# Attention row maxima: of three products a key tile, one made of 256 keys in each row half

## Chip, core and metric

The kernel runs on one core of a Trainium2 chip. The metric is the device time of one execution in microseconds; the time shown is the median of three runs. The core has five engines that run side by side and wait for each other by semaphores: TensorE (PE, its weight loads PEld), VectorE (DVE), ScalarE (ACT), GpSimd (POOL) and SyncE (SP, which issues DMAs). TensorE writes into PSUM, eight banks of 128 rows by 512 f32 columns.

## The reference

A pre-norm transformer block on 2048 tokens of width 640, all in f32: 32 heads of width 20, then a gated feed-forward layer of width 1728.

```
h   = x + attention(layernorm(x))
out = h + ffn(layernorm(h))

scores = einsum("bhqd,bhkd->bhqk", q, k) * (Dh ** -0.5)
p = softmax(scores, axis=-1)
o = einsum("bhqk,bhkd->bhqd", p, v)
ffn(x) = (silu(x @ w_gate) * (x @ w_up)) @ w_down
```

The softmax is the exact one: the row maximum over all 2048 keys is taken off before the exponential. The maxima are computed from q and k by products of their own, ahead of the scores that they serve.

## The kernel before

The program has three stages: layer norm and projections, attention, then output projection and feed-forward. The order of the work is written out by hand; every engine runs its instructions in the order in which the program issues them.

Attention is cut into 32 units `u`: eight groups of four heads, times four chunks of 512 queries. A unit runs over 16 key tiles `kt` of 128 keys, so there are 512 tiles. The keys and queries of four heads lie in two row halves (`b`, partitions 0 to 63 and 64 to 127) of two pairs each; a head uses 60 rows, and two more rows carry the negated row maximum in two parts. A product that has 60 or 62 rows uses one half of TensorE's rows.

In a key tile (`ORDER`, a string of letters) stand:

- `s` and `S`: a score product (line 1300, `scores`), 62 rows by 128 keys against 512 queries into one bank of `ps_one`, in row half 0 and 1; two of each. ScalarE takes the exponential of each bank into `probs` (line 1306).
- `m` and `M`: a maximum product (line 274, `max_one`), 60 rows by 128 queries against 512 keys into one bank of `ps_max`, in row half 0 and 1; three in all, `m` twice in even tiles and `M` twice in odd ones. VectorE reduces each bank to one column of `mx` (line 280). They serve a later unit: the list `rest` holds 736 entries (unit, key chunk, query tile, pair), each with both halves.
- `W`: the weighing of the tile two back (line 1310, `weigh`): four heads side by side in four column strips, into the bank `acc`. After the sixteenth tile of a unit ScalarE copies `acc` to `o` (line 1320).

`ps_one` has four banks in turn, so each score of a tile waits for the exponential of the score at the same place in the tile before. `ps_max` has three; the one whose reduction came first is given out first. A bank is given out when the product that fills it is issued, and that product carries the wait. When a unit has all its maxima, `max_all` reduces the columns of `mx` to one value per row (line 287), GpSimd splits it in two parts, VectorE turns it and DMAs bring it into the queries' spare rows. `W` also carries other work by the piece, among it the preparation of feed-forward weights on GpSimd, and in the last two units products of the output projection, which take `ps_max` banks.

```
def next_max(b):
    if singles[b]:
        a = singles[b].pop(0)
        max_one(*a)
```

After some 491 tiles the maxima are used up and a tile is `sSsSW`.

Of the kernel before, what the change touches and what calls it, by code (L numbers as in the profile page):

```python
# [9 lines left out]
F32 = mybir.dt.float32  # L10
# [4 lines left out]
ALU = mybir.AluOpType  # L15
AX = mybir.AxisListType

P = 128
S = 2048
D = 640  # L20
H = 32
# [4 lines left out]
CH = 512  # L26
NC = S // CH
TPC = CH // P
# [9 lines left out]
LOWEST = -3.4028234e38  # L38
GD = G * DH

ORDER = ("WsSmmSsM", "WSsMMsSm")


@with_exitstack
def tile_block(ctx: ExitStack, tc: tile.TileContext, x, wqkv, wo, wg, wu, wd, out):
    nc = tc.nc
# [100 lines left out]
    NU = NG * NC  # L147
# [4 lines left out]
    stk = att_ctx.enter_context(tc.tile_pool(name="stk", bufs=1, side="right"))  # L152
    k_stk = [stay.tile([P, 2, S], F32R, name="k_stk0", tag="first")]
    v_stk = [stay.tile([P, NT, VG], F32, name="v_stk0", tag="second")]
    keys, queries, values = {}, {}, {}
# [24 lines left out]
    def load_keys(g, cs):  # L180

        k = keys[g] = k_stk[g % 2]
        stack(k[:, :, cs], 1, g, cs.start // CH)
# [11 lines left out]
        )  # L195

    def mx_tile(u, **tag):
        return stk.tile([P, 2, 2, TPC, NC], F32, name=f"mx{u}", **tag)

    mxs = {u: mx_tile(u) for u in range(NU) if u % NC < 2 or u == 2}  # L200

# [63 lines left out]

        return differences, maxima

    def max_one(u, kc, t, pair, b):

        ps = ps_max()  # L270
        if u not in mxs:
            mxs[u] = mx_tile(u, tag="mx_late", bufs=3)
        rows = slice(b * ROW, b * ROW + NPART)
        nc.tensor.matmul(  # L274
            ps,
            queries[u][rows, pair, t * P : (t + 1) * P],
            keys[u // NC][rows, pair, kc * CH : (kc + 1) * CH],
            start=True, stop=True,
        )
        nc.vector.tensor_reduce(  # L280
            mxs[u][:, b, pair, t, kc : kc + 1], ps, axis=AX.X, op=ALU.max
        )

    def max_all(u):

        ends[u] = stk.tile([P, G * TPC], F32, name="neg", tag="neg", bufs=2)
        nc.vector.tensor_reduce(
            ends[u], mxs[u].rearrange("p b h t k -> p (b h t) k"), axis=AX.X, op=ALU.max, negate=True
        )

    def max_parts(u):

        neg = ends[u]
        both = ends[u] = stk.tile([P, 2, G * TPC], F32R, name="neg2", bufs=2)
        nc.gpsimd.tensor_copy(both[:, 0], neg)
        nc.gpsimd.tensor_tensor(
            out=both[:, 1], in0=neg, in1=both[:, 0].bitcast(F32), op=ALU.subtract
        )
# [66 lines left out]
    with tc.tile_pool(name="pa", bufs=2) as pa:  # L365
# [21 lines left out]
        slot = [0]  # L387
# [468 lines left out]
        for c in range(NC):  # L856
# [7 lines left out]
            for j, (kind, *which) in enumerate(work):  # L864
# [31 lines left out]
                else:  # L896
# [10 lines left out]
                    def ps_max():  # L907
                        n = turn[0] % 5
                        turn[0] += 1
                        if n > 2:  # L910
                            return psum_two.tile([P, CH], F32, name="ps_max", tag="ps_two")
                        return psum.tile([P, CH], F32, name="ps_max", tag="ps_max", bufs=3)
# [4 lines left out]
                if (c, j) in ((1, 14), (1, 16), (2, 4), (3, 4)):  # L917
                    n = c if c > 1 else (j - 14) // 2
# [376 lines left out]
    def scores(u, kt, j, probs):  # L1295

        p, b = divmod(j, 2)
        rows = slice(b * ROW, b * ROW + NPART + 2)
        ps = ps_one()
        nc.tensor.matmul(  # L1300
            ps,
            keys[u // NC][rows, p, kt * P : (kt + 1) * P],
            queries[u][rows, p, :],
            start=True, stop=True,
        )
        nc.scalar.activation(probs[p][:, b, :], ps, AF.Exp, scale=scale)  # L1306
# [43 lines left out]
            )  # L1350

    todo, tail, accs, later, full, now = [], [], {}, {}, [], [0]
    singles = [[(*a, b) for a in rest] for b in range(2)]
    left = {u: sum(2 for a in rest if a[0] == u) for u in range(1, NU)}

    def next_max(b):
        if singles[b]:
            a = singles[b].pop(0)
            max_one(*a)
            left[a[0]] -= 1  # L1360
            if left[a[0]] == 0:
                full.append(a[0])

    def weigh_next():
        u, kt, probs = todo.pop(0)
        if kt == 0:
            accs[u] = psum.tile([P, CH], F32, name="acc", tag=f"ps_{last % 3}")
        weigh(u, kt, probs, accs[u])
        if kt == NT - 1:
            queues = [nc.sync] if u + 1 < NU else [nc.scalar, nc.sync]  # L1370
            tail.append((u, *row_sums(accs.pop(u), *queues)))

    extra = []
    preparing = prepare_weights()
    for u in range(NU):
        g, c = divmod(u, NC)
        if g == NG - 1 and c >= 2:
            _, first, ln, flips, _ = ahead
            extra = [*first, *ln, lambda: None, *flips]
        for kt in range(NT):  # L1380
            now[0] = u * NT + kt
            probs = [pp.tile([P, 2, CH], F32, name="probs") for _ in range(2)]
            heads = [[0, 2], [1, 3]]
            order = ORDER[now[0] % 2] if singles[0] or singles[1] else "sSsSW"
            for op in order:
                if op in "mM":
                    next_max(int(op == "M"))
                elif op in "sS":
                    scores(u, kt, heads[op == "S"].pop(0), probs)
                else:  # L1390
                    if len(todo) == 2:
                        weigh_next()
                    for f in later.pop(now[0], ()):
                        f()
                    if extra:
                        extra.pop(0)()
                    if preparing and u and kt not in (3, 4):
                        preparing.pop(0)()
                    if now[0] == (NU - NC) * NT + 8:
                        unit_ring, last_ring = weight_rings()  # L1400
# [52 lines left out]
    u, o, r = tail.pop()  # L1453
# [561 lines left out]
```

## Time and profile before

| | us |
|---|---|
| median of three runs | 2027.66 (2025.42 to 2028.07) |
| the profiled execution | 2025.84 |
| its span, first to last instruction | 2024.0 |
| TensorE busy | 2003.7 |
| VectorE busy | 1602.4 |
| ScalarE busy | 1439.9 |
| GpSimd busy | 788.5 |

The mean granted clock of TensorE is 0.999. Rows of groups give line, engine, operation, what is written from what, shape and count, then busy us, mean ns of one, and the idle time before them with what ended it. Rows of windows give the stretch, then the busy time of PE, PEld, DVE, ACT and POOL with counts, the clock, the DMA share and GB/s. Rows of the timeline give start, length, engine and line; "x4" merges neighbours, and the end of a matmul is modelled, so starts are what to read on PE. Rows of one source line give the duration in ns as least, median and most. An instruction's weights are loaded by a row of PEld, which carries its waits.

### The profile page before, as it was taken

What the parts mean: (1) busy time and instruction counts of PE and PEld (TensorE: products, weight loads), DVE (VectorE), ACT (ScalarE), POOL (GpSimd) and SP (SyncE); (2) the same over time, 40 slices, a digit from 0 to 9 for tenths busy, and PEclk for the clock granted to TensorE, in tenths of its full rate; (3) what the DMA queues carried; (4) which work ended last, traced back from release to release, by engine and by line L of the source; (5) the groups of instructions that cost most, each with busy time, mean ns of one, the idle gap of its engine ahead of it and who ended that gap; (6) DMA issues with size and microseconds to landing.
All of it is one profiled execution on the core that took longest, in us unless ns stands there. A gap on an engine that the chain in (4) does not pass through costs nothing. (4 is left out here: it accounts for less than half of the span.)

```text
span 2024.0 us, 39916 instructions
## 1 busy us (share of the span) xinstructions
PE 2003.7 (99%) x14302; PEld 1242.0 (61%) x14302; DVE 1602.4 (79%) x2816; ACT 1439.9 (71%) x2827; POOL 788.5 (39%) x1166
## 2 busy tenths in 40 slices
PE   8999999999999999999999999999999999999999
PEld 6999995333334333333333333345588888888888
DVE  5687778888888898988988988875387666676677
ACT  4678878999999999999999999987633222212221
POOL 7464423334443453443400011011155444744555
PEclk9999999999999999999999999999999999999999
DMA  7877563443634544435412132221258654974642
GB/s 245 255 254 261 180 207 83 117 146 95 189 104 139 153 143 128 155 128 173 148 58 68 36 85 58 80 63 56 59 182 296 218 189 154 353 268 159 204 150 95
DMA packets 199340, 310.35 MB, mean 153 GB/s; under 512 B 53744, under 2 KB 87856, under 8 KB 198120
## 3 DMA queue, kind: packets, MB, share of 16 engines
q1 hardware_dynamic: 192552, 284.21, 43.7%
q0 software_dynamic: 6496, 23.60, 3.9%
q8 instruction: 114, 1.87, 0.4%
q14 instruction: 82, 0.67, 0.1%
q10 hardware_dynamic: 96, 0.00, 0.0%
HBM read 208.11 MB, written 99.19 MB: 152 GB/s over the span
## 5 line engine op out<-in xcount | busy, mean ns | idle before, releaser
L1306 ACT ACTIVATE probs<-ps_one 128x512 f32<-128x512 f32 x2048 | 1056.6, 615 | 61.2 <-PE ps_one L1300 35.3
L280 DVE TENSOR_REDUCE mx<-ps_max 128x1 f32<-128x512 f32 x1472 | 924.9, 684 | 106.3 <-PE ps_one L1300 77.6
L1300 PE MATMUL ps_one<-q_stk,k_stk 62*128 62x512 f32 x2048 | 583.3, 450 | 0.7 <-DMA q_stk<-m_d 0.6
L1310 PE MATMUL acc<-probs,v_stk 128*32 128x512 f32 x4096 | 546.2, 606 | 0.0
L1300 PEld LDWEIGHTS ps_one<-q_stk,k_stk 62*128 62x128 f32 x2048 | 248.7, 184 | 441.2 <-ACT probs L1306 416.7
L274 PE MATMUL ps_max<-k_stk,q_stk 60*128 60x512 f32 x1472 | 374.9, 426 | 1.0 <-DVE mx L261 0.9
L274 PEld LDWEIGHTS ps_max<-k_stk,q_stk 60*128 60x128 f32 x1472 | 272.8, 186 | 26.9 <-DVE mx L280 2.1
L1693 DVE TENSOR_TENSOR tmp<-ps_a,tmp 128x512 f32<-128x512 f32 x208 | 141.2, 689 | 122.4 <-PE ps_a L1478 96.7
L261 DVE TENSOR_REDUCE mx<-ps_max 128x2 f32<-128x512 f32 x288 | 180.7, 685 | 63.9 <-PE ps_max L239 58.7
L1310 PEld LDWEIGHTS acc<-probs,v_stk 128*32 128x32 f32 x4096 | 80.6, 108 | 179.0 <-issue 168.0
L251 ACT ACTIVATE ps_max<-ps_max 128x512 f32<-128x512 f32 x288 | 151.6, 584 | 42.9 <-PE ps_max L239 40.3
L1572 PE MATMUL ps_b<-halves,yp 128*128 128x320 f32 x1032 | 179.0, 308 | 1.5 <-DMA halves<-j_d 1.2
L1572 PEld LDWEIGHTS ps_b<-halves,yp 128*128 128x128 f32 x1032 | 165.2, 188 | 17.5 <-POOL yp L90 1.5
L1478 PE MATMUL ps_a<-t,units 128*128 128x512 f32 x624 | 162.5, 396 | 0.0
L90 POOL TENSOR_TENSOR yp<-y,yp 128x256 fp32r<-128x256 f32 x96 | 60.2, 627 | 189.8 <-ACT yp L89 189.8
L1478 PE MATMUL ps_a<-z,units 128*128 128x512 f32 x516 | 133.9, 394 | 0.0
L1478 PEld LDWEIGHTS ps_a<-t,units 128*128 128x128 f32 x624 | 112.6, 188 | 18.5
L1345 POOL TENSOR_TENSOR o<-o,rb 128x512 f32<-128x512 f32 x31 | 39.9, 1286 | 199.1 <-DMA q_stk<-q_d 74.1
L1577 DVE TENSOR_TENSOR h<-ps_b,h 128x320 f32<-128x320 f32 x248 | 109.9, 480 | 6.9 <-PE ps_b L1572 5.4
L643 PE MATMUL ps_one<-z_hi,w_lo 64*128 64x512 f32 x380 | 113.5, 392 | 0.0
L643 PE MATMUL ps_one<-z_lo,w_hi 64*128 64x512 f32 x380 | 112.3, 392 | 0.0
L643 PE MATMUL ps_one<-z_hi,w_hi 64*128 64x512 f32 x380 | 111.7, 393 | 0.0
(225 smaller groups left out, 2637.4 us busy)
## 6 DMA issues: line engine op xcount, KB each, us to landing
units<-w_d SPq DMA_DIRECT2D x186, 256.0 KB
w_d<-stage SPq DMA_DIRECT2D x106, 256.0 KB
halves<-j_d SPq DMA_DIRECT2D x70, 320.0 KB
j_d<-stage SPq DMA_DIRECT2D x42, 320.0 KB
k_stk<-k_d SPq DMA_DIRECT2D x64, 160.0 KB
q_stk<-q_d SPq DMA_DIRECT2D x64, 160.0 KB
raw<-k_d SPq DMA_DIRECT2D x62, 160.0 KB
raw<-q_d SPq DMA_DIRECT2D x54, 160.0 KB
```

Source lines behind the costliest of these rows:

```text
L251: nc.scalar.activation(ps, ps, AF.Relu)
L261: nc.vector.tensor_reduce(mx[:, b, :, t, kc], ps.rearrange("p (j n) -> p j n", j=2), axis=AX.X, op=ALU.max,)
L274: nc.tensor.matmul(ps, queries[u][rows, pair, t * P : (t + 1) * P], keys[u // NC][rows, pair, kc * CH : (kc + 1) * CH], start=True, stop=True,
L280: nc.vector.tensor_reduce(mxs[u][:, b, pair, t, kc : kc + 1], ps, axis=AX.X, op=ALU.max)
L643: nc.tensor.matmul(ps, a[rows], b[rows], start=(i == n == 0), stop=(i == 1 and n == last), skip_group_check=True,)
L1300: nc.tensor.matmul(ps, keys[u // NC][rows, p, kt * P : (kt + 1) * P], queries[u][rows, p, :], start=True, stop=True,)
L1306: nc.scalar.activation(probs[p][:, b, :], ps, AF.Exp, scale=scale)
L1310: nc.tensor.matmul(acc[32 * j : 32 * j + 32, :], values[u // NC][:, kt, j * VW : j * VW + 32], probs[j // 2][:, j % 2, :], start=(kt == 0) ...
L1478: nc.tensor.matmul(ps.rearrange("p (t n) -> p t n", t=TPC), w[k][:, i], z[k][:, :, j], start=(first and m == 0), stop=(last and m == len(n ...
L1572: nc.tensor.matmul(ps, a, b, start=(n == 0), stop=(n == len(pairs) - 1))
L1577: nc.vector.tensor_tensor(out=h, in0=ps, in1=h, op=ALU.add)
L1693: add = lambda out, ps, x: nc.vector.tensor_tensor(out=out, in0=ps, in1=x, op=ALU.add)
```

## The change

One of the three maximum products of a tile is split in two. `h` and `H` issue a product of 256 keys each, `h` in row half 0, `H` in row half 1, into the two halves of one bank of `ps_max`; the bank is taken at `h`, and after `H` one reduction over two groups of 256 columns writes the maxima of both halves. An entry of the list needs two such banks, one for the first 256 keys and one for the other 256. The two remaining products are one whole entry, first half 1, then half 0. Since two row halves write the same bank, `H` is made to wait until `h` has ended: a no-op on TensorE that waits for TensorE's own semaphore, and then the product.

The first 256 keys of an entry use the slot of its key chunk in `mx`; the maxima of the other 256 go to one of two extra slots per row, so `mx` grows from 4 to 6 slots for all units but the first. The extra slots are filled with the lowest f32: 16 tiles by GpSimd ahead of attention, the other 15 by VectorE when they are first used.

```diff
-ORDER = ("WsSmmSsM", "WSsMMsSm")
+ORDER, LAST_ORDER = "WhSsMsSHm", "sSsSW"
...
     def mx_tile(u, **tag):
-        return stk.tile([P, 2, 2, TPC, NC], F32, name=f"mx{u}", **tag)
+        n = NC + (2 if tag else u > 0)
+        return stk.tile([P, 2, 2, TPC, n], F32, name=f"mx{u}", **tag)
...
+    def max_product(ps, u, t, pair, b, k0, k1):
         rows = slice(b * ROW, b * ROW + NPART)
         nc.tensor.matmul(
             ps,
             queries[u][rows, pair, t * P : (t + 1) * P],
-            keys[u // NC][rows, pair, kc * CH : (kc + 1) * CH],
-            start=True, stop=True,
+            keys[u // NC][rows, pair, k0:k1],
+            start=True, stop=True, skip_group_check=True,
         )
...
+    def max_slots(u):
+        if u not in mxs:
+            mxs[u] = mx_tile(u, tag="mx_late", bufs=3)
+            nc.vector.memset(mxs[u][:, :, :, :, NC:], LOWEST)
+        return mxs[u]
...
+    def max_half(ps, i, u, kc, t, pair, b):
+        k0 = kc * CH + i * (CH // 2)
+        cols = slice(b * CH // 2, (b + 1) * CH // 2)
+        max_product(ps[:, cols], u, t, pair, b, k0, k0 + CH // 2)
+
+    def max_halves(ps, i, u, kc, t, pair):
+        slot = kc
+        if i:
+            n = halved[u, t, pair] = halved.get((u, t, pair), 0) + 1
+            slot = NC - 1 + n
         nc.vector.tensor_reduce(
-            mxs[u][:, b, pair, t, kc : kc + 1], ps, axis=AX.X, op=ALU.max
+            max_slots(u)[:, :, pair, t, slot], ps.rearrange("p (j n) -> p j n", j=2),
+            axis=AX.X, op=ALU.max,
         )
...
     def next_max(b):
-        if singles[b]:
-            a = singles[b].pop(0)
+        if not whole and rest:
+            a = rest.pop(0)
+            whole.extend((*a, i) for i in (b, 1 - b))
+        if whole:
+            a = whole.pop(0)
             max_one(*a)
...
+    def next_half(b):
+        if not halves_of and rest:
+            a = rest.pop(0)
+            halves_of.extend((i, a, []) for i in range(2))
+        if not halves_of:
+            return
+        i, a, banks = halves_of[0]
+        if not banks:
+            banks.append(ps_max())
+            max_half(banks[0], i, *a, b)
+        else:
+            nc.tensor.keepalive_nop([nc.tensor.lower_ap(banks[0])])
+            max_half(banks[0], i, *a, b)
+            max_halves(banks[0], i, *a)
+            counted(a[0], 2 * i)
+            halves_of.pop(0)
...
+    for u in range(1, NU):
+        if u in mxs:
+            nc.gpsimd.memset(mxs[u][:, :, :, :, NC:], LOWEST)
```

TensorE's order in one tile of the middle of attention, with the number behind a name telling one bank from another and the engine whose semaphore is waited for in brackets: before, the weighing, then two scores, two maximum products, two scores, a maximum product.

```order
L1310 MATMUL acc_15791<-probs_15752,v_stk1_5606 32x512 x2
L1310 MATMUL acc_15791<-probs_15753,v_stk1_5606 32x512 x2
L1300 MATMUL ps_one_15827<-q_stk_14413,k_stk1_5605 128x512 [waits Activation_49]
L1300 MATMUL ps_one_15830<-q_stk_14413,k_stk1_5605 128x512 [waits Activation_49]
L274 MATMUL ps_max_15833<-k_stk1_5605,q_stk_15434 128x512 [waits DVE_49]
L274 MATMUL ps_max_15836<-k_stk1_5605,q_stk_15434 128x512 [waits DVE_49]
L1300 MATMUL ps_one_15839<-q_stk_14413,k_stk1_5605 128x512 [waits Activation_49]
L1300 MATMUL ps_one_15842<-q_stk_14413,k_stk1_5605 128x512 [waits Activation_49]
L274 MATMUL ps_max_15845<-k_stk1_5605,q_stk_15434 128x512 [waits DVE_49]
```

The same place of the changed kernel (its lines 1338, 1328 and 272 are the weighing, the scores and the maximum products):

```order
L1338 MATMUL acc_20514<-probs_20745,v_stk1_5606 32x512 x2
L1338 MATMUL acc_20514<-probs_20746,v_stk1_5606 32x512 x2
L272 MATMUL ps_max_20810<-k_stk1_5605,q_stk_20162 128x256 [waits DVE_49]
L1328 MATMUL ps_one_20812<-q_stk_19135,k_stk1_5605 128x512 [waits Activation_49]
L1328 MATMUL ps_one_20815<-q_stk_19135,k_stk1_5605 128x512 [waits Activation_49]
L272 MATMUL ps_max_20818<-k_stk1_5605,q_stk_20162 128x512 [waits DVE_49]
L1328 MATMUL ps_one_20821<-q_stk_19135,k_stk1_5605 128x512 [waits Activation_49]
L1328 MATMUL ps_one_20824<-q_stk_19135,k_stk1_5605 128x512 [waits Activation_49]
L272 MATMUL ps_max_20810<-k_stk1_5605,q_stk_20162 128x256 [waits PE_49,PE_sequencer_49]
L272 MATMUL ps_max_20830<-k_stk1_5605,q_stk_20162 128x512 [waits DVE_49]
```

The first half product now opens the tile's products, the second stands next to last, behind the fourth score and behind the no-op, and the last whole product follows it. The whole products and the scores alternate between the halves.

VectorE's order of reductions in the changed kernel, with the two-column one (line 307) between the whole ones (line 292); before, all rows were alike:

```order
L292 TENSOR_REDUCE mx21_139<-ps_max_16066 128x1 [waits PE_49]
L307 TENSOR_REDUCE mx21_139<-ps_max_16058 128x2 [waits PE_sequencer_49,PE_49]
L292 TENSOR_REDUCE mx21_139<-ps_max_16078 128x1 [waits PE_49]
L292 TENSOR_REDUCE mx21_139<-ps_max_16102 128x1 [waits PE_49]
L307 TENSOR_REDUCE mx21_139<-ps_max_16094 128x2 [waits PE_sequencer_49,PE_49]
L292 TENSOR_REDUCE mx21_139<-ps_max_16114 128x1 [waits PE_49]
```

The bank of the two half products (16058) is taken before that of the first whole one (16066) but reduced after it. The number of reductions per tile is the same as before.

More of the change, by code (lines that the diff above doesn't have):

```diff
@@ L266, in max_four @@
         return differences, maxima
[L268 to L272, printed above, removed]
+    def max_product(ps, u, t, pair, b, k0, k1):
         rows = slice(b * ROW, b * ROW + NPART)
@@ L276, in max_one @@
             queries[u][rows, pair, t * P : (t + 1) * P],
-            keys[u // NC][rows, pair, kc * CH : (kc + 1) * CH],
-            start=True, stop=True,
-        )
+            keys[u // NC][rows, pair, k0:k1],
+            start=True, stop=True, skip_group_check=True,
+        )
+    halved = {}
+    def max_slots(u):
[3 more added lines that the diff above has]
+        return mxs[u]
+    def max_one(u, kc, t, pair, b):
+        ps, mx = ps_max(), max_slots(u)
+        max_product(ps, u, t, pair, b, kc * CH, (kc + 1) * CH)
+        nc.vector.tensor_reduce(mx[:, b, pair, t, kc : kc + 1], ps, axis=AX.X, op=ALU.max)
+    def max_half(ps, i, u, kc, t, pair, b):
[7 more added lines that the diff above has]
+            slot = NC - 1 + n
+            assert slot < max_slots(u).shape[-1]
         nc.vector.tensor_reduce(
-            mxs[u][:, b, pair, t, kc : kc + 1], ps, axis=AX.X, op=ALU.max
+            max_slots(u)[:, :, pair, t, slot], ps.rearrange("p (j n) -> p j n", j=2),
+            axis=AX.X, op=ALU.max,
         )
@@ L1352, in tile_block, with counted @@
     todo, tail, accs, later, full, now = [], [], {}, {}, [], [0]
-    singles = [[(*a, b) for a in rest] for b in range(2)]
     left = {u: sum(2 for a in rest if a[0] == u) for u in range(1, NU)}
-    def next_max(b):
-        if singles[b]:
-            a = singles[b].pop(0)
-            max_one(*a)
-            left[a[0]] -= 1
-            if left[a[0]] == 0:
-                full.append(a[0])
+    whole, halves_of = [], []
+    def counted(u, n):
+        left[u] -= n
+        if n and left[u] == 0:
+            full.append(u)
+    def next_max(b):
+        if not whole and rest:
[3 more added lines that the diff above has]
+            a = whole.pop(0)
+            max_one(*a)
+            counted(a[0], 1)
+    def next_half(b):
[14 more added lines that the diff above has]
+            halves_of.pop(0)
     def weigh_next():
@@ L1383, in tile_block @@
             heads = [[0, 2], [1, 3]]
-            order = ORDER[now[0] % 2] if singles[0] or singles[1] else "sSsSW"
-            for op in order:
+            for op in ORDER if rest or whole or halves_of else LAST_ORDER:
                 if op in "mM":
                     next_max(int(op == "M"))
+                elif op in "hH":
+                    next_half(int(op == "H"))
                 elif op in "sS":
```

## Prediction

> **What bounds the kernel now.** I read the table of windows first, because the page's shares average over stages with different limits, and the change touches one stage alone: attention with row maxima.
>
> ```profile
> 300.00:1347.00 1047.00, 1045.34 (x7386) 420.92 (x7386) 933.39 (x1552) 1015.34 (x1985) 321.95 (x526) 1.00 0.38 113
> 1347.00:1392.00 45.00, 44.94 (x288) 28.08 (x282) 31.01 (x68) 27.01 (x53) 7.42 (x5) 1.00 0.25 81
> L1306 ACT ACTIVATE probs<-ps_one 128x512 f32<-128x512 f32 x2048 | 1056.6, 615 | 61.2 <-PE ps_one L1300 35.3
> L280 DVE TENSOR_REDUCE mx<-ps_max 128x1 f32<-128x512 f32 x1472 | 924.9, 684 | 106.3 <-PE ps_one L1300 77.6
> L274 PE MATMUL ps_max<-k_stk,q_stk 60*128 60x512 f32 x1472 | 374.9, 426 | 1.0 <-DVE mx L261 0.9
> ```
>
> From 300 to 1347 us TensorE counts as busy nearly throughout and ScalarE for 97% of the stretch, so shares do not say which of them sets the pace. The timeline of one key tile does (columns: start, us, engine, line).
>
> ```profile
> 799.51 0.50 PE L1300 MATMUL ps_one<-q_stk,k_stk 62*128 62x512 f32 x2
> 799.84 0.40 PE L274 MATMUL ps_max<-k_stk,q_stk 60*128 60x512 f32 x1
> 799.85 0.39 PE L1300 MATMUL ps_one<-q_stk,k_stk 62*128 62x512 f32 x1
> 800.09 0.51 PE L274 MATMUL ps_max<-k_stk,q_stk 60*128 60x512 f32 x2
> 800.32 0.40 PE L1300 MATMUL ps_one<-q_stk,k_stk 62*128 62x512 f32 x1
> 800.64 1.06 PE L1310 MATMUL acc<-probs,v_stk 128*32 128x512 f32 x8
> 801.64 0.50 PE L1300 MATMUL ps_one<-q_stk,k_stk 62*128 62x512 f32 x2
> 800.04 2.07 ACT L1306 ACTIVATE probs<-ps_one 128x512 f32<-128x512 f32 x4
> 800.28 1.89 DVE L280 TENSOR_REDUCE mx<-ps_max 128x1 f32<-128x512 f32 x3 [0.24 <-PE ps_one L1300]
> ```
>
> Products start in pairs, one per row half, a slot of 0.24 us apart (799.84 to 800.32 is two). Seven products fill seven of eight places: one row half is empty in the fourth slot. The tile's products take 1.13 us (799.51 to 800.64), the weighing 1.00 (to 801.64), the tile 2.13. In that 1.13 the first slot is 0.10 longer, since nothing hides its weight load, and 0.09 passes after the last slot. Four exponentials end 2.07 us after the first began; with 0.62 for the first, below, the others come at 0.48 each, and ScalarE needs 1.93 us a tile. VectorE's three reductions take 1.89 after an idle 0.24. So TensorE sets the 2.13, with ScalarE 0.2 us behind it.
>
> Once per sixteen tiles ScalarE also copies the accumulator:
>
> ```profile
> 733.48 0.63 ACT L1320 ACTIVATE o<-acc 128x512 f32<-128x512 f32 x1
> 801.49 0.62 ACT L1306 ACTIVATE probs<-ps_one 128x512 f32<-128x512 f32 x1
> 801.96 0.63 ACT L1320 ACTIVATE o<-acc 128x512 f32<-128x512 f32 x1
> 802.44 2.12 ACT L1306 ACTIVATE probs<-ps_one 128x512 f32<-128x512 f32 x4
> 804.61 0.18 PEld L1300 LDWEIGHTS ps_one<-q_stk,k_stk 62*128 62x128 f32 x1 [0.30 <-ACT probs L1306]
> 805.04 0.16 PEld L1310 LDWEIGHTS acc<-probs,v_stk 128*32 128x32 f32 x8 [0.24 <-issue]
> 806.03 0.19 PEld L1300 LDWEIGHTS ps_one<-q_stk,k_stk 62*128 62x128 f32 x2 [0.84 <-ACT probs L1306]
> ```
>
> Two copies are 68.48 us apart, two sets of sixteen tiles: 34.24 us a set, 0.16 over 16 x 2.13. This place also shows what comes next: with ScalarE 0.48 late (801.96 to 802.44), its fourth exponential ends at 804.56, the next tile's fourth score, which takes that bank, goes out at 804.61, and the weighing starts 0.43 later. Fourth exponential to fourth score is the wait to watch.
>
> **The change, part by part.** *Half a slot off TensorE.* Each tile now has, in either row half, two scores, one whole maximum product and one of 256 keys: 3.5 slots and no empty place. The length of a 256-key product is seen in the projection stage, where the same halves are used:
>
> ```profile
> 250.54 0.39 PE L643 MATMUL ps_one<-z_hi,w_hi 64*128 64x512 f32 x1
> 250.77 0.48 PE L239 MATMUL ps_max<-raw 60*128 60x256 f32 x4
> 251.01 0.39 PE L643 MATMUL ps_one<-z_hi,w_hi 64*128 64x512 f32 x1
> ```
>
> Four of them, two per half, fit into 0.24 us: 0.12 each, half a slot, with the weight load hidden. TensorE alone would need 2.13 - 0.12 = 2.01 us a tile.
>
> *What is late next: the fourth score's bank.* In its half the first and fourth score now have only one product between them; its weights could go out when that product starts, 0.34 us into the tile rather than 0.58. The fourth exponential of the tile before ends 0.53 + 2.07 = 2.60 us after that tile's start (799.51 to 800.04 is the 0.53), and 0.05 passes before the weight load. At 2.01 us a tile that is 0.64 into the next, 0.30 too late. Today there is cover: 2.65 - 2.13 = 0.52, before 0.58. So the pace becomes a ring over two tiles: start of a tile to its first exponential 0.53, four exponentials 2.07, hand-over 0.05, fourth score to weighing 0.43 as at 804.61, plus 0.12 for the second half product that follows in the same row half, weighing 1.00. Sum 4.20, or 2.10 a tile. Of the 0.12 saved, 0.03 is left.
>
> *TensorE's wait on itself.* The second half product writes the bank of the first and must see it ended. The first is the tile's first product and ends about 0.4 us into the tile (0.39 is the longest 256-key product of that stage), the wait is reached only behind the fourth score, at 2.65 - 2.10 = 0.55. Nothing is waited for; the instruction itself remains, and it stands ahead of the second half product and the last whole one, and then of the weighing.
>
> ```profile
> L1300 PEldq EVENT_SEMAPHORE  x64: 51/51/692, 319.0 to 1404.6; - x64
> L239 PE MATMUL ps_max<-raw,raw x608: 271/278/389, 68.1 to 304.8; 60*128 60x256 f32 x152
> ```
>
> The nearest such instructions run 0.05 us when their semaphore is there. Below, 0.05 is the cost; above, no row of before shows a wait of TensorE on itself, and I bound it by 0.25, a 0.05 run plus the first slot's unhidden 0.10 twice. I take 0.10: the run and one hand-over of 0.05. Behind it the last whole product needs 0.43, so that way is 0.53 beside 0.43 + 0.12 = 0.55: hidden by 0.02. Up to 0.12 it costs nothing, beyond that half of the excess per tile.
>
> *Banks and VectorE.* There are three reductions a tile as before, over the same 512 columns each; the one over two halves writes two columns, and 128x2 reductions took as long:
>
> ```profile
> L261 DVE TENSOR_REDUCE mx<-ps_max 128x2 f32<-128x512 f32 x288 | 180.7, 685 | 63.9 <-PE ps_max L239 58.7
> L287 DVE TENSOR_REDUCE neg<-mx 128x16 f32<-128x64 f32 x8 | 1.7, 214 | 0.1
> ```
>
> The first half product takes the bank whose reduction came first, some 0.6 us before it is wanted. The last whole product takes the one reduced last: 800.28 + 1.89 is 2.66 after the tile's start, 2.71 with a hand-over; its turn comes at 2.65 + 0.10 = 2.75. Cover 0.04; the ring through that bank is 2.71 + 0.43 + 1.00 = 4.14, 0.06 below the other. The final maximum reads 96 columns for 64: 0.11 longer at most (half of 214 ns), once per sixteen tiles, against 0.24 idle per tile. The fills of the two extra slots (16 on GpSimd ahead of the stage, 15 on VectorE) are once per sixteen tiles too, cost less than such a reduction each, and hide in the same idle time; GpSimd is 31% busy. No DMA is added or moved.
>
> *The copy.* Its 0.48 us now lands on the ring. Today it costs 0.16; all of it would be 0.48; ScalarE has 2.10 - 1.93 = 0.17 spare a tile to catch up, so I take 0.30.
>
> *The sum.* A set of sixteen: 16 x 2.10 + 0.30 = 33.90 against 34.24, a gain of 0.34. The late tiles are these:
>
> ```profile
> L1306 ACT ACTIVATE probs<-ps_one 128x512 f32<-128x512 f32 x49 | 25.3, 608 | 18.0 <-PE ps_one L1300 17.9
> L274 PE MATMUL ps_max<-k_stk,q_stk 60*128 60x512 f32 x32 | 9.7, 433 | 0.0
> ```
>
> From 1347 to 1392 us 32 products, 11 tiles, run beside the output projection; ScalarE idles there, so the whole 0.12 comes off: 1.3 us. The other 1472/3 - 11 = 480 tiles are 30 sets: 10.2 us. Together 11.5. The profiled run, 2025.84 us (span 2024.0 and 1.84 around it), would become 2014.3; it stands 1.8 below the median 2027.66, so I forecast 2016.2 as the median.
>
> **Rivals.** *A, slower: products start strictly in program order.* Then the last whole product cannot start before the second half product, which stands behind the fourth score in the other half: 0.53 + 2.07 + 0.05 + 0.10 + 0.24 + 0.24 + 0.09 + 1.00 = 4.32, 2.16 a tile, 16 x 2.16 + 0.30 = 34.86 a set, +0.62 x 30 = +18.6, nothing gained late: 2046. It decides as soon as the order is strict. Against it: at 800.09 the third maximum product starts, though the fourth score at 800.32 stands ahead of it in the program; the halves run past each other. Chance 0.07. The Trainium skill, in "TensorE: Matmul & The Clock Gate", Part 3, "The mechanism", says that matmuls start and end in program order and only weight loads are pulled ahead; by that rule this change gains nothing, and the rows at 800.09 and 800.32 speak against it.
>
> *B, slower: the self-wait is dear.* From (34.24 - 0.30)/16 = 2.12 a tile, a ring of 4.24 and 0.16 us in place of 0.10, the gain is gone. At the bound of 0.25 the ring is 0.53 + 2.07 + 0.05 + 0.25 + 0.43 + 1.00 = 4.33, 34.94 a set, +21.0 - 1.3: 2047. For it: nothing in this trace prices the round trip. Against it: the semaphore is long there. Chance 0.13.
>
> *C, much faster: the fourth score does not wait,* because exponentials come sooner than the row says. Then TensorE's 2.01 holds: 16 x 2.01 + 0.30 = 32.46, -53.4 - 1.3: 1973. Against it: the wait is seen at 804.61. Chance 0.07.
>
> *D, nothing to measure: the cover on the last bank is gone* and VectorE's third reduction holds the last product. From 0.06 us late it decides; at 0.10 late the ring is 4.14 + 0.10 = 4.24, 2.12 a tile, 34.22 a set: -0.6 - 1.3, 2026. For it: the cover is the smallest of all; against it, the reductions do not change in size. Chance 0.14.
>
> **How the numbers follow.** The forecast has the remaining 0.59; its own range is 2007 (ring 2.09, the copy at 0.16) to 2021 (self-wait 0.14). About 0.2%, 4 us, is what a measurement of this kernel can tell from no change. Faster: forecast and C, 0.66; same: D, 0.14; slower: A and B, 0.20. The range leaves out C and the dearer part of A and B: 2004 to 2035.
>
> **What would show it.** In the profile after: tiles of two lengths in turn, about 2.0 and 2.2 us, instead of one; the fourth score's weight load waiting for ScalarE in about every second tile, 0.2 us or more; half products 0.12 us long; the last whole maximum starting before the second half product or with it. A wait for TensorE itself that ends last would mean B; the last product never ahead of the second half, A; ScalarE without idle time at under 2.05 us a tile, C; the last product released by VectorE, D. I am wrong in kind if the tile stays at 2.13 or grows.

## The result, and the profile after

The changed kernel took 2041.18 us (median of 4 runs, 2037.66 to 2042.14) beside 2027.87 for the kernel before (2025.42 to 2029.81): a ratio of 1.0072, 95% interval 1.0059 to 1.0084. The forecast was 2016.2, a gain; the change loses 0.7%. The profiled run took 2037.66, span 2035.8, mean granted clock 0.999.

The table of windows, for the stretch shown of before and the late tiles:

```profile
300.00:1347.00 1047.00, 1035.91 (x7772) 441.69 (x7770) 926.16 (x1550) 997.97 (x1963) 322.36 (x541) 1.00 0.37 112
1357.00:1405.00 48.00, 48.00 (x323) 30.38 (x319) 33.34 (x72) 30.42 (x60) 7.53 (x5) 1.00 0.27 89
```

TensorE, busy for 1045.34 of these 1047 us before, is now idle for 11.09 of them, and ScalarE gets through 1963 instructions in the stretch where it had done 1985. Tiles of the usual kind are not the cause. Two of them, in the timeline of TensorE and of its weight loads:

```profile
797.38 0.38 PE L272 MATMUL ps_max<-k_stk,q_stk 60*128 60x256 f32 x1
798.06 0.44 PE L272 MATMUL ps_max<-k_stk,q_stk 60*128 60x512 f32 x2
798.42 1.06 PE L1338 MATMUL acc<-probs,v_stk 128*32 128x512 f32 x8
799.42 0.38 PE L272 MATMUL ps_max<-k_stk,q_stk 60*128 60x256 f32 x1
800.57 1.06 PE L1338 MATMUL acc<-probs,v_stk 128*32 128x512 f32 x8
801.57 0.38 PE L272 MATMUL ps_max<-k_stk,q_stk 60*128 60x256 f32 x1
797.61 0.46 PEld L1328 LDWEIGHTS ps_one<-q_stk,k_stk 62*128 62x128 f32 x2
800.03 0.18 PEld L1328 LDWEIGHTS ps_one<-q_stk,k_stk 62*128 62x128 f32 x1 [0.19 <-ACT probs L1334]
```

A tile starts with its first half product: 797.38, 799.42, 801.57, so one tile takes 2.04 us and the next 2.15, together 4.19. In the first the fourth score's weights follow the third's without a gap (797.61), in the second they go out 0.19 late, released by ScalarE. That is the ring over two tiles.

What is new stands in the table of waits (engine and line, what ended the wait, us in total, times, longest) and in the row of the no-op's line:

```profile
PEld ps_one L1328 <- ACT probs L1334: 59.5, 254, 1.2
PEld acc L1338 <- issue: 133.3, 487, 3.3
L1411 PEldq EVENT_SEMAPHORE  x492: 51/51/51, 320.3 to 1403.1; - x164
```

The fourth score waits for ScalarE 254 times, in about every second tile. The no-op's 51 ns do not tell whether it waited: in this trace every semaphore instruction of TensorE that waits for one semaphore has a record of 51 ns. Its starts do. In 63 of 492 cases it starts within 50 ns of the end of the first half product, as if released there; in the others that product had ended earlier. Of the 63, 54 lie in the 477 tiles counted below, and these are among the shortest, 2.01 us on average. So nothing here shows that TensorE's wait for itself makes a tile longer. But the weights of the weighing wait up to 3.3 us for nothing that the profile shows. Before, the same row had a longest wait of 0.7:

```profile
PEld acc L1310 <- issue: 168.0, 482, 0.7
```

One such place in the timeline of after:

```profile
389.13 0.39 PE L272 MATMUL ps_max<-k_stk,q_stk 60*128 60x256 f32 x1
390.19 0.15 PEld L1338 LDWEIGHTS acc<-probs,v_stk 128*32 128x32 f32 x6 [0.25 <-issue]
390.20 1.05 PE L1338 MATMUL acc<-probs,v_stk 128*32 128x512 f32 x5
392.87 1.05 PE L1338 MATMUL acc<-probs,v_stk 128*32 128x512 f32 x3 [1.62 <-issue]
392.87 0.14 PEld L1338 LDWEIGHTS acc<-probs,v_stk 128*32 128x32 f32 x2 [2.53 <-issue]
393.85 0.38 PE L272 MATMUL ps_max<-k_stk,q_stk 60*128 60x256 f32 x1
```

The tile that starts at 389.13 takes 4.72 us. TensorE stops in the middle of a weighing, behind six of eight weight loads, and no other engine is named as what it waits for. There are eight such long tiles, at 389, 489, 623, 702, 806, 874, 1220 and 1320 us, 3.00 to 5.10 us long. Counted in TensorE's recorded instructions (weight loads, matmuls and no-ops), seven of the eight stops come at the same place modulo 256, behind the 193rd. Only the one at 702 does not: it is the first tile of a unit, and its scores wait 1.06 us for the DMA that brings the turned maxima into the queries' spare rows. The number 256 points to the loading of the program itself. The page lists DMA queue 8 (packets, MB, share) as carrying instructions; of before, then of after:

```profile
q8 instruction: 114, 1.87, 0.4%
```

```profile
q8 instruction: 120, 1.97, 0.4%
```

TensorE has 29,207 recorded instructions before and 30,690 after; divided by 256 these are 114.1 and 119.9, the packets of the queue. So each packet is a block of 256 of its instructions. Before, a packet starts as TensorE passes a border (0.2 us ahead of it at the median, 3.7 behind it at most) and brings the block behind the next border. After, it starts 9.6 us behind the border at the median, and up to 16.2 us. At 33 instructions and 2.10 us a tile a block lasts 256/33 x 2.10 = 16.3 us, so a packet that late starts about when its block is needed. The packets of the seven stops start 14.3 to 16.2 us behind their border, and TensorE goes on 2.4 to 3.3 us after the packet's start: in the place shown the packet starts at 389.53 and TensorE goes on at 392.87.

The account of the first 477 tiles with maxima, from the starts of their first products (1021.0 us before, 1031.9 after):

| | before | after | difference, us |
|---|---|---|---|
| usual tile | 2.125 | 2.098 | 477 x -0.027 = -12.9 |
| longer tiles, us over the usual one | 36 of 2.30, one of 2.98: 7.3 | 14 of 2.34, 22 of 2.45, 12 of 2.52: 16.0 | +8.7 |
| the eight very long ones, over the usual | none | 8 x (4.015 - 2.098) | +15.3 |

The sum is +11.1, measured +10.9.

### The profile page after: what moved, and what is told of

Read it like the earlier page. It is cut to its first block, busy times and chain, and to the rows that moved or that the text cites. A ratio compares the mean times of both kernels' runs of the same rounds, so it can differ in the third digit from the quotient of the medians.

```text
span 2035.8 us, 41923 instructions
## 1 busy us (share of the span) xinstructions
PE 2003.5 (98%) x14794; PEld 1268.9 (62%) x14794; DVE 1604.5 (79%) x2831; ACT 1434.5 (70%) x2827; POOL 790.3 (39%) x1182
## 5 line engine op out<-in xcount | busy, mean ns | idle before, releaser
L292 DVE TENSOR_REDUCE mx<-ps_max 128x1 f32<-128x512 f32 x980 | 672.4, 686 | 110.4 <-PE ps_max L272 84.2
L272 PE MATMUL ps_max<-k_stk,q_stk 60*128 60x512 f32 (+1 forms) x1964 | 579.0, 378 | 3.0 <-issue 1.9
L1328 PE MATMUL ps_one<-q_stk,k_stk 62*128 62x512 f32 x2048 | 545.4, 436 | 1.3 <-DMA q_stk<-m 1.1
L272 PEld LDWEIGHTS ps_max<-k_stk,q_stk 60*128 60x128 f32 x1964 | 248.9, 185 | 407.5 <-DVE mx L307 253.2
L1328 PEld LDWEIGHTS ps_one<-q_stk,k_stk 62*128 62x128 f32 x2048 | 301.0, 185 | 81.8 <-ACT probs L1334 59.5
L307 DVE TENSOR_REDUCE mx<-ps_max 128x2 f32<-128x512 f32 x492 | 336.3, 684 | 5.0 <-PE ps_max L272 2.8
L262 DVE TENSOR_REDUCE mx<-ps_max 128x2 f32<-128x512 f32 x288 | 180.8, 685 | 64.4 <-PE ps_max L240 60.5
```

Source lines behind the costliest of these rows:

```text
L262: nc.vector.tensor_reduce(mx[:, b, :, t, kc], ps.rearrange("p (j n) -> p j n", j=2), axis=AX.X, op=ALU.max,)
L272: nc.tensor.matmul(ps, queries[u][rows, pair, t * P : (t + 1) * P], keys[u // NC][rows, pair, k0:k1], start=True, stop=True, skip_group_ch ...
L292: nc.vector.tensor_reduce(mx[:, b, pair, t, kc : kc + 1], ps, axis=AX.X, op=ALU.max)
L307: nc.vector.tensor_reduce(max_slots(u)[:, :, pair, t, slot], ps.rearrange("p (j n) -> p j n", j=2), axis=AX.X, op=ALU.max,)
L1328: nc.tensor.matmul(ps, keys[u // NC][rows, p, kt * P : (kt + 1) * P], queries[u][rows, p, :], start=True, stop=True,)
```

## The experiments

Two theories stood after this profile. One: the no-op makes the blocks of instructions late, and the ring costs what was forecast. The other: the loss comes with the products (more instructions per tile, or the ring). Later runs ask which property of the no-op does it. For each profile I took, between 330 and 1340 us, the time from TensorE's passing of a border (behind the 193rd of every 256 instructions) to the start of the packet of queue 8 that belongs to it. The times are medians of all runs; a ratio is to the kernel before in the same series of runs, whose median lay between 2024.77 and 2027.87, so kernels are compared by their ratios:

| run | median us | ratio (95% interval) | packet behind border, median / most us |
|---|---|---|---|
| before | 2027.87 | 1 | -0.2 / 3.7 |
| changed kernel | 2041.18 | 1.0072 (1.0059 to 1.0084) | 9.6 / 16.2 |
| e1, the no-op alone | 2039.92 | 1.0069 (1.0052 to 1.0085) | 10.3 / 14.9 |
| e2, the half products alone | 2026.16 | 1.0001 (0.9992 to 1.0011) | 0.0 / 2.5 |
| e3, the wait on VectorE | 2026.87 | 1.0004 (0.9995 to 1.0013) | 0.0 / 3.1 |
| e4, the ring shortened | 2014.51 | 0.9945 (0.9931 to 0.996) | 1.5 / 3.8 |
| e5, e3 and e4 | 2012.36 | 0.9933 (0.9917 to 0.9949) | 0.1 / 3.4 |
| e6, a no-op in every fourth tile | 2025.15 | 1.0001 (0.9991 to 1.001) | 0.0 / 4.3 |
| e7, the no-op earlier | 2024.52 | 0.9996 (0.9983 to 1.0009) | 1.9 / 5.7 |
| e8, the no-op of e1, earlier | 2050.55 | 1.0125 (1.0105 to 1.0145) | 0.9 / 3.6 |
| e9, no wait, a query tile named | 2315.25 | 1.1437 (1.1409 to 1.1465) | 10.0 / 25.5 |
| e10, no wait | 2031.7 | 1.0031 (1.0019 to 1.0043) | 11.0 / 18.0 |
| e11, no wait, earlier | 2027.47 | 1.0003 (0.9994 to 1.0013) | 0.8 / 3.4 |
| e12, no wait, later | 2032.94 | 1.0043 (1.0026 to 1.006) | 11.6 / 15.9 |

**e1: the no-op alone.** The kernel before, with a no-op ahead of each third maximum product, behind the fourth score, on a bank filled a tile ago.

```diff
     def max_one(u, kc, t, pair, b):
+        maxima[0] += 1
+        if maxima[0] % 3 == 0 and maxima[1] is not None:
+            nc.tensor.keepalive_nop([nc.tensor.lower_ap(maxima[1])])
         ps = ps_max()
+        if maxima[0] % 3 == 0:
+            maxima[1] = ps
```

> The kernel before with one thing added: ahead of every third maximum product a no-op on TensorE that waits for a semaphore already reached, and the product waits for the no-op; products, banks and reductions are those of before. Theory F (the semaphore instruction in each tile makes the fetch of TensorE's next instruction block start late): the tile stays at 2.13 us, block transfers start 4 to 15 us after the block border in attention instead of within 1 us, some 5 to 10 stalls of 1 to 3 us appear in the weighing, in all 10 to 18 us slower, 2038 to 2046. Rival N (more products and instructions per tile are what makes the fetch late): no stall, 2026 to 2030.

The loss is as large as the change's, the usual tile stays at 2.13 (434 of mean 2.131), and the packets are late. But the expected stops are missing: at 31 instructions and 2.13 us a tile a block lasts 17.6 us, the latest packet comes 14.9 us behind its border, and the profile shows no stop at a border. So the total came out as expected for another reason, and what lateness costs, this run doesn't tell. Of the 13.8 us lost in 477 tiles, 1.6 lie in the first, 7.5 in nine tiles (eight of 2.94 us, one of 4.04) in which the third product waits for VectorE, probably because the no-op names a bank, and the rest is spread over the others. One of the nine:

```profile
393.58 0.18 PEld L1307 LDWEIGHTS ps_one<-q_stk,k_stk 62*128 62x128 f32 x1
394.52 0.18 PEld L281 LDWEIGHTS ps_max<-k_stk,q_stk 60*128 60x128 f32 x1 [0.75 <-DVE mx L287]
```

**e2: the half products alone.** The kernel before, its third maximum product made as two of 256 keys in the same row half, without a no-op.

```diff
-        nc.tensor.matmul(ps, ..., keys[u // NC][rows, pair, kc * CH : (kc + 1) * CH], ...)
+        parts = 2 if maxima[0] % 3 == 0 else 1
+        for i in range(parts):
+            n = CH // parts
+            nc.tensor.matmul(ps[:, i * n : (i + 1) * n], ..., keys[...][rows, pair, kc * CH + i * n : kc * CH + (i + 1) * n], ...)
```

> The kernel before with every third maximum product made as two of 256 keys, one after the other in the same row half and into the same bank, without a wait: one product and one weight load more per tile, no semaphore instruction. Theory F: block transfers on time, no stall, 2026 to 2031 (the row half that got the second weight load has an empty slot beside it). Rival N: late transfers and stalls as in the changed kernel, 2036 to 2046.

Nothing is lost and the packets are on time: two more instructions a tile, a load and a product, leave the packets on time where the single no-op made them late.

**e3: the same products, the wait on another engine.** The changed kernel without the no-op on TensorE; VectorE waits for the first half product instead, and TensorE for VectorE.

```diff
             max_half(banks[0], i, *a, b)
+            nc.vector.keepalive_nop([nc.vector.lower_ap(banks[0])])
         else:
-            nc.tensor.keepalive_nop([nc.tensor.lower_ap(banks[0])])
             max_half(banks[0], i, *a, b)
```

> The changed kernel with the self-wait moved: VectorE's sequencer waits for the first half product, and the second half product waits for VectorE's sequencer; TensorE has no semaphore instruction in the tile. Theory F: block transfers within about 1 us of the border, no stall in the weighing, the tile at 2.10 as in the changed kernel; the changed kernel less its 14.5 us of stalls, 2023 to 2029. Rival N: stalls stay, 2037 to 2044. If the hand-over from VectorE is dearer than the no-op by over 0.1 us, the tile is 2.13 or longer and the time 2028 or more without any stall.

The packets are on time, and no stop at a border is left; the 477 tiles take 1018.4 us, 2.6 less than before. The gain is given back in the late tiles, which now take 4.55 and 5.07 us in turn: VectorE's wait stands behind its other work there, and TensorE behind it. VectorE's timeline of such a place:

```profile
1371.89 0.49 DVE L1065 TENSOR_TENSOR h<-ps_max,h 128x320 f32<-128x320 f32 x1 [1.73 <-PE ps_max L1059]
1376.97 0.49 DVE L1065 TENSOR_TENSOR h<-ps_max,h 128x320 f32<-128x320 f32 x1 [2.01 <-PE ps_max L1059]
1381.51 0.49 DVE L1065 TENSOR_TENSOR h<-ps_max,h 128x320 f32<-128x320 f32 x1 [1.74 <-PE ps_max L1059]
```

**e4: the ring shortened.** The changed kernel with the second half product ahead of the fourth score, so that nothing stands in that row half between fourth score and weighing; the no-op goes along.

```diff
-ORDER, LAST_ORDER = "WhSsMsSHm", "sSsSW"
+ORDER, LAST_ORDER = "WhSsMsHSm", "sSsSW"
```

> The changed kernel with the second half product ahead of the fourth score instead of behind it, self-wait and all else as they are. Theory R (the tile's pace is a ring over two tiles through the fourth score's bank, and the half product behind that score lengthens it by 0.12 us): the ring falls to 4.08, and the one through VectorE's third reduction, 4.14, takes over: 2.07 us a tile in place of 2.10, about 0.8 us a set of sixteen under the changed kernel's sets without stalls, some 15 to 24 us off in all: 2017 to 2027, stalls of the instruction fetch still there. Rival P (the order does not matter, the pairs of 2.01 and 2.19 have another cause): the tiles stay as they are, 2037 to 2043.

The usual tile falls to 2.082 (433 of them), as a shorter ring should make it, though by less than the 0.06 that 0.12 off the ring would give. The total, 2014.51, missed the expected 2017 to 2027 from below: the no-op stands in every tile here too, yet the packets are on time and the stops are gone. Its weight loads show tiles that are all alike:

```profile
805.41 0.18 PEld L272 LDWEIGHTS ps_max<-k_stk,q_stk 60*128 60x128 f32 x1 [0.84 <-DVE mx L307]
806.05 0.19 PEld L1328 LDWEIGHTS ps_one<-q_stk,k_stk 62*128 62x128 f32 x1
806.50 0.16 PEld L1338 LDWEIGHTS acc<-probs,v_stk 128*32 128x32 f32 x8 [0.26 <-issue]
807.49 0.18 PEld L272 LDWEIGHTS ps_max<-k_stk,q_stk 60*128 60x128 f32 x1 [0.84 <-DVE mx L307]
```

The fourth score goes out 0.64 into the tile, no longer late in every second one, and the weighing follows 0.45 behind, where it was 0.54 in the changed kernel (800.03 to 800.57). What the shorter ring alone is worth shows beside e7 below, whose packets are on time too: 1009.5 us for the 477 tiles, where e7 takes 1019.5.

**e5: both.** The order of e4 and the wait on VectorE, except in the last two units, where the no-op on TensorE stays and the late tiles take 4.48.

```diff
-ORDER, LAST_ORDER = "WhSsMsSHm", "sSsSW"
+ORDER, LAST_ORDER = "WhSsMsHSm", "sSsSW"
...
+            if now[0] < (NU - 2) * NT:
+                nc.vector.keepalive_nop([nc.vector.lower_ap(banks[0])])
         else:
-            nc.tensor.keepalive_nop([nc.tensor.lower_ap(banks[0])])
+            if now[0] >= (NU - 2) * NT:
+                nc.tensor.keepalive_nop([nc.tensor.lower_ap(banks[0])])
```

> The same order, and the wait moved onto VectorE's sequencer except in the last two units, where the self-wait stays. Theories F and R together: no stall and 2.07 us a tile, 16 x 2.07 + 0.35 = 33.5 us a set against 34.24, 30 sets: 22 us under the kernel before, less some 3 us for the tiles in which other work meets the ring: 2002 to 2011. If F holds and R does not, as the kernel with the wait on VectorE alone: 2024 to 2029.

This has the lowest median, with a usual tile of 2.070, and misses the expected bounds by 1.4 us. It and e4, whose intervals overlap, are the only versions that are faster than the kernel before.

**e6: one no-op in four tiles.** The kernel of e1 with `% 12` in place of the first `% 3`.

> The kernel before with the no-op in every fourth tile only. If a semaphore instruction holds the fetch back only near itself, transfers are late by less than the 8.5 us between two of them, the interval between transfers spreads less than with one in every tile (standard deviation 6.6 us there, 1.3 before), no stall of over 0.5 us is left, 2025 to 2031. If any such instruction within a block holds the fetch until the block is nearly used up, stalls of 1 to 3 us stay, 2033 to 2042.

On time, nothing lost: one no-op in four tiles is too few to make the packets late. What lies between that and every tile was not run.

**e7: the no-op one product earlier.** The changed kernel, products unmoved; the no-op is issued ahead of the fourth score.

```diff
-ORDER, LAST_ORDER = "WhSsMsSHm", "sSsSW"
+ORDER, LAST_ORDER = "WhSsMsnSHm", "sSsSW"
...
         else:
-            nc.tensor.keepalive_nop([nc.tensor.lower_ap(banks[0])])
             max_half(banks[0], i, *a, b)
...
+                elif op == "n":
+                    if halves_of and halves_of[0][2]:
+                        nc.tensor.keepalive_nop([nc.tensor.lower_ap(halves_of[0][2][0])])
```

> The changed kernel with its products in the changed order; only the no-op is issued one product earlier, ahead of the fourth score in place of behind it. Theory P (place): the no-op makes the instruction blocks late only where it stands behind the tile's last product that waits for ScalarE; ahead of it the blocks come on time (intervals 12 to 22 us, standard deviation under 2), no stall over 0.5 us, tiles of 2.0 and 2.2 in turn with mean 2.10 as before, total 2023 to 2029. Rival Q (order): it was the place of the second half product, not of the no-op, that mended the blocks in the run with the half ahead of the score; then the stalls stay, 5 or more of them of 0.7 us or longer, total 2037 to 2043.

This prices the lateness. The instructions are those of the changed kernel, one of them moved by one product. The usual tile is the same (2.099). The median was 13.3 us above the kernel before (2041.18 and 2027.87) and is now 0.3 below it (2024.52 and 2024.83 in this series), which makes 13.6 us. Between the two profiles the seven tiles that stopped at a border differ by 13.8 us, all 477 tiles together by 12.5. The long stop is out of the row of waits:

```profile
PEld acc L1338 <- issue: 121.7, 482, 0.4
```

The eighth tile, at 702 us in the changed kernel, is still 1.3 us longer than before (3.44): here too its scores wait for the DMA of the maxima, 0.99 us.

**e8: the no-op of e1, ahead of the tile's first maximum product** (`% 3 == 1`, naming the second product's bank, for `% 3 == 0` and the third's).

> The kernel before with a no-op in every tile as in the run with the no-op alone, but ahead of the first maximum product of the tile in place of the third, on a bank whose reduction is over by then. Theory P (place): ahead of the last product that waits for ScalarE it makes no block late: standard deviation of the intervals under 2, no stall over 0.5 us, tile 2.12 to 2.14, total 2024 to 2030. Rival Q (any place): the same stalls as with the no-op ahead of the third product, standard deviation 5 or more, total 2037 to 2043.

The packets are on time. The total missed: the usual tile is 2.183, since the second maximum product waits for VectorE, some 0.2 us a tile, probably because the no-op holds a bank longer and the banks come round in another order:

```profile
PEld ps_max L281 <- DVE mx L287: 107.5, 460, 0.9
```

**e9 and e10: a no-op that waits for nothing**, at the place of e1. In e9 it names the first unit's query tile:

```diff
+            nc.tensor.keepalive_nop([nc.tensor.lower_ap(queries[0])])
```

> The kernel before with a no-op in every tile at the place that made the blocks late, ahead of the third maximum product, but naming a tile that was written long ago, so that it neither waits for a semaphore nor is waited for. Theory V (wait): the semaphore makes the difference, blocks on time, 2024 to 2030. Rival I (instruction): one more instruction at that place is enough, whatever it waits for: standard deviation 5 or more, stalls, 2037 to 2043.

The packets are late, but the total says nothing: the edit kept one of four query buffers in use, and later units waited for their queries.

```profile
PE ps_one L1307 <- DMA q_stk<-m_d: 142.1, 20, 13.8
```

So e10 names a constant instead (`ident` for `queries[0]`):

> The kernel before with a no-op in every tile ahead of the third maximum product, as in the run without a wait, but naming a constant of the program, since there the named query tile was kept alive and the loads of later queries waited for its buffer. It waits for nothing and nothing waits for it. Theory I (instruction): one more instruction at this place makes the blocks late whatever it waits for: a median of 8 to 12 us between the passing of a block border and the next block's transfer, tile 2.12 to 2.14, total 2034 to 2044. Rival V (wait): only a no-op with a semaphore does it; median under 2 us, total 2024 to 2030.

The packets are late, though the no-op waits for no semaphore and no product waits for it (in the trace it only counts one up): it is the instruction, not its wait. The total, +5.5 us, lies between the two expectations, since lateness costs only where it comes near a block's time, here 17.6 us as in e1. In the profile it does so once, at 1308 us, with a packet 18.0 us late; the stop stands behind a weighing (columns as before):

```profile
1308.14 1.07 PE L1315 MATMUL acc<-probs,v_stk 128*32 128x512 f32 x8
1311.60 0.50 PE L1305 MATMUL ps_one<-q_stk,k_stk 62*128 62x512 f32 x2 [2.38 <-issue]
```

**e11 and e12: the same bare no-op ahead of the fourth score, and ahead of the weighing.**

```diff
                 elif op in "sS":
+                    if order != "sSsSW" and not heads[op == "S"][1:] and not heads[op != "S"]:
+                        nc.tensor.keepalive_nop([nc.tensor.lower_ap(ident)])
```

> The same no-op, one product earlier: ahead of the fourth score. Theory P (place): the blocks come on time, median under 3 us after the border, tile 2.12 to 2.14, total 2024 to 2031. Rival Q: late as behind it, 2034 to 2044.

```diff
         u, kt, probs = todo.pop(0)
+        if singles[0] or singles[1]:
+            nc.tensor.keepalive_nop([nc.tensor.lower_ap(ident)])
```

> The same no-op, behind the third maximum product and ahead of the weighing. Theory P (place): it too stands behind the tile's last product that waits for ScalarE, so the blocks are late, median 8 to 12 us, 2034 to 2044. Rival T: only a no-op directly behind the fourth score does it; then median under 3 us and 2024 to 2031.

Ahead of the score the packets are on time and the total is that of before; ahead of the weighing they are late, and the total is 1 us short of the expected bounds. The profile there, of the fastest of four runs (2028.38 to 2036.39), has two short stops at a border, which make their tiles 0.8 and 0.5 us longer, behind packets 15.9 and 15.5 us late. In the whole series the packets are late in the kernels that have a no-op in every tile behind the last product that waits for ScalarE, and in no other.

## Why the prediction was wrong

**The step that failed** is "TensorE's wait on itself". It read "Up to 0.12 it costs nothing", and gave the no-op a price as a wait. As a wait it costs nothing that the runs show: the tiles in which it is released as the first half product ends are among the shortest, 2.01 us. But an instruction at that place makes the program's own blocks late, and this cost 13.8 us between the profiles of the changed kernel and e7, and 13.6 between their medians, each beside its kernel before. No term and no rival held it; B had the direction, a dear self-wait, and its 2047 is within 6 us, but by another mechanism, so that this nearness is luck. The Trainium skill, in "Runtime: NRT & Kernel Launch", "Instruction fetch mechanics", says that instructions come in blocks of 256, that the next is fetched while the current one is executed, and that crossing a border is mostly hidden. The runs agree with the blocks and, in the kernel before, with the hiding; in the changed kernel seven of 61 packets in the stage were not hidden.

**The pace was right.** Ring forecast 4.20 us for two tiles, 2.10 each; measured 4.19 in the tiles shown and 2.098 over 421. Tiles of two lengths, the fourth score waiting in every second one, and the last whole product starting at 798.06, ahead of the second half product (798.22 in the single records that the row at 798.06 merges), came as described. e4 speaks for the ring from the other side, since the tile shortens when the 0.12 behind the fourth score is taken away; what holds that tile at 2.08, where a ring of 4.08 would give 2.04, was not settled. In the rows of e4 the fourth score's weights go out without a wait, so the ring through that score no longer decides there.

**The copy and its like were mis-sized.** The copy's tile is 0.35 longer than the usual one where 0.30 was taken, near enough. Missing was ScalarE's other work, which lands on the ring too. Once in four units ScalarE writes the turned maxima `m` of a later unit, 0.27 us, and the tile with it, 0.25 over the usual one before, is 0.39 over it now:

```profile
419.51 0.27 ACT L89 ACTIVATE m<-ps_one 16x128 fp32r<-16x128 f32 x1
419.94 2.07 ACT L1334 ACTIVATE probs<-ps_one 128x512 f32<-128x512 f32 x4 [0.16 <-PE ps_one L1328]
```

The longer tiles together cost 8.7 us more than before; the term held 30 x (0.30 - 0.16) = 4.2. With the pace at -12.9 for -14.4, and the late tiles at 4.48 for 4.53 (0.05 each where 0.12 was taken), and the eighth long tile at 1.5, this leaves some 3 us of the gain of 11.5 without the stops. e7, which is that kernel, has a span 3.1 us below that of before (2020.9), and over all its runs a ratio of 0.9996: no difference. So of the 23.3 us between the forecast (11.5 less) and the profile (a span 11.8 longer), 13.8 are the stops and some 8.4 these terms; about 1 is left unassigned.

**The rivals.** A is refuted by the start at 798.06, C by the 254 waits. D: the last whole product's weights never wait for VectorE in the usual tile; e8 shows what it is like when a maximum product does (2.18 a tile). B's dear self-wait is refuted by the usual tile, 2.098 where its bound gives 2.165, and by the tiles of 2.01 us.

## What to carry to other kernels

An added instruction has a place as well as a duration: when a tuned engine shows stops of microseconds "for nothing", count its instructions modulo 256 and set the instruction queue's packets beside the borders. Where an engine must wait for itself, try the wait at another place of its stream, or on an engine with nothing else to do there, before giving up the change. And when an edit makes another engine's ring the bound, price all of that engine's small jobs, not the largest alone.

## What the runs showed of the hardware

- A block of 256 TensorE instructions starts to come as the engine passes the border one block ahead, 14.6 to 21.7 us between packets (before). With a no-op behind the fourth score in every tile it starts 10 us later at the median, and the packets are 5.0 to 28.2 us apart (changed kernel); with the same no-op one product earlier, 10.7 to 22.4 (e7). Why an instruction there delays the transfer was not found; that the no-op need not wait for a semaphore (e10, e12), that the count of instructions is not the reason (e2), and that one no-op in four tiles does not do it (e6), is shown.
- The stops come when the lateness nears a block's time. With a block of 16.3 us seven packets 14.3 to 16.2 us late meant a stop (changed kernel); with 17.6 us one of 18.0 did (e10), two of 15.9 and 15.5 made short ones (e12), and 14.9 made none (e1). In none of these profiles does TensorE run a block sooner than 2.2 us after its packet's start. That lateness and these 2 us together must stay under a block's time is the likely rule, argued from these runs, not tested by varying the block's time alone.
- Products of different row halves start out of program order: 798.06 ahead of 798.22, and so in 476 of 488 tiles of the changed kernel. The Trainium skill's "TensorE: Matmul & The Clock Gate", Part 3, "The mechanism", has starts in program order; the measurement decides.
